# The low part of the last weight quarter made by accumulating transfers from GpSimd instead of VectorE, with the factor 4096 of the parts moved to y's side

## The chip, the cores and the metric

The kernel runs on one core of one Trainium2 chip. The metric is device time in microseconds (us) of one execution. A profiled execution also leaves a trace, whose span is the time from its first to its last instruction.

## The reference

Two blocks follow each other. The first is a Mamba-2 state-space scan over `x` of shape (4, 8, 768, 32) with decays `a` and state size 16; its output `y`, read as 3072 tokens of 256 features, is the input of the second, a feed-forward block with a hard-swish in place of a gate:

```
h = x @ w_in                      # 3072x256 @ 256x2048
g = h * np.clip(h + 3.0, 0.0, 6.0) / 6.0
out = (g @ w_out).astype(np.float32)   # 3072x2048 @ 2048x256
```

Inputs `w_in` and `w_out` arrive as 64-bit floats and are decoded to 32-bit ones on the chip.

## The kernel before, in words

The sequence is cut into six chunks of 128 positions (`NC` = 6), each with its four batches, so 512 tokens a chunk. Step `k` of the main loop runs the feed-forward block of chunk `k` and, interleaved by hand, the scan of chunk `c = k + 1` and preparations for `ahead = k + 2`. All engines work through queues in the order in which the code issues instructions; a queue stops at an instruction whose inputs are not ready, and everything behind it waits too. SyncE (SP) issues the loads and stores; GpSimd (POOL) issues no transfer.

Chunk 0 multiplies `w_in` in plain 32-bit floats (`mlp_in`). From chunk 1 on, TensorE multiplies in the faster `float32r` type, and the lost precision is brought back by parts. Each of y and `w_in` is split into a high part `hi` (a rounded, scaled copy made by ScalarE), a low part `lo` (what the rounding lost, plus a small multiple) and `less` (a combination of the two). One tile `h` of 128 features by 512 tokens is then the sum of hi·hi, lo·lo and less·less with a factor 4097 between them (`squares`, `enlarge`, `cross`). Each of the three is two products of 128x512, one for each half `j` of the 256 input features.

`w_in` has four quarters, held in tiles `w_in[0..3]` of 128 partitions by 2 x 512 floats. The generator `in_parts(i)` makes the parts of quarter `i`. Its pieces are issued by `next(ins[i])`: the first call issues the two ScalarE instructions for `hi` (L663); the second issues two VectorE instructions of 128x512 for half 0, `lo` (L666) and `less` (L669); the third the same for half 1. For quarters 0 to 2 that happens before step 1. For quarter 3 the three calls stand in step 1, after tiles f = 4, 5 and 7 of the 16 tiles of `h`. Quarter 3 serves f = 12 to 15.

In step 1, tile f goes through these pieces: `squares(f)` (TensorE, four products, hi first and then lo), `cross(f - 2)` (TensorE, two products with `less`), `enlarge(f)` (ScalarE, L711), `factor(f - 2)`, which is a ScalarE `ramp` (L730) and a VectorE product (L735) into `gT`. Six PSUM banks hold the tiles `h` in turn, so `squares(12)` needs that L735 of f = 6 is done. `conceal` (L158) issues the GpSimd selects on the decay tile `L` after f = 8 and f = 12; `weight_sums` (L776) puts VectorE sums of 128x1024 after f = 9, 11 and 13; `g_sums` (L796) issues sums of `gT` on GpSimd after f = 15. The SP queue loads for later chunks are issued around the start of step 1: `L` (L301), `eto` (L308), `xt` (L119) and `B` (L94).

`split_y(k)` makes the three parts of y: `y_hi` on ScalarE (L680), `y_lo` (L681) and `y_less` (L684) on VectorE, two instructions of 128x512 each per chunk.

Of the kernel before, what the change touches and what calls it, by code (L numbers as in the profile page):

```python
# [8 lines left out]
FP32 = mybir.dt.float32  # L9
# [4 lines left out]
AF = mybir.ActivationFunctionType  # L14
ALU = mybir.AluOpType
# [6 lines left out]
def kernel(  # L22
# [24 lines left out]
    nc = tc.nc  # L47
# [7 lines left out]
    NK = DM // P  # L55
# [30 lines left out]
    def load_bc(c):  # L86

        sl = slice(c * P, (c + 1) * P)  # L90

        def tokens_first(src, queue=nc.sync, **where):
            t = loads.tile([P, NB * NH, N], FP32, **where)
            queue.dma_start(out=t, in_=src[:, :, sl, :].rearrange("b h s n -> s (b h) n"))  # L94
            return t

        def pairs_first(src):
            t = loads.tile([P, 2, NB, 4, N], FP32, name="pairs", tag="bc")
            for b in range(NB):
                for h in range(2):  # L100
                    nc.sync.dma_start(  # L101
                        out=t[:, h, b].rearrange("s a n -> s (a n)"),
                        in_=src[b, h:NH:2, sl, :].rearrange("h (s a) n -> h s (a n)", a=4))
            return t

        if 0 < c < TURN:
            bcs[c] = [tokens_first(C, name="C", tag="bc")]
        Bs[c] = tokens_first(B, nc.scalar if c == 0 else nc.sync, name="B", bufs=1)
        if c == 0:
            bcs[c] = [pairs_first(C), Bs[c]]  # L110
        elif c < TURN:
            bcs[c].append(Bs[c])
        else:
            bcs[c] = [pairs_first(C), pairs_first(B)]

    def load_x(c):
        sl = slice(c * P, (c + 1) * P)
        xts[c] = loads.tile([P, NB * NH, D], FP32, name="xt", bufs=1)
        nc.sync.dma_start(out=xts[c], in_=x[:, :, sl, :].rearrange("b h s d -> s (b h) d"))  # L119

    NP = 4
    FP = NF // NP
    w_in = [const.tile([P, NK, FP * P], FP32, name="w_in", tag=f"w{i}") for i in range(NP)]
# [31 lines left out]
    def conceal_in(t, pattern):  # L155
# [24 lines left out]
        out=head, in_=head, pattern=[[-2 * N, NQ], [-N, 2]], compare_op=ALU.is_ge,  # L180
        fill=0.0, base=0, channel_multiplier=1)
    nc.gpsimd.affine_select(
        out=head, in_=head, pattern=[[2 * N, NQ], [N, 2]], compare_op=ALU.is_ge,
# [59 lines left out]
    less = const.tile([P, G], BF16, name="less")  # L243
# [134 lines left out]
    def conceal(c, p):  # L378
        conceal_in(Ls[c][:, 2 * p:2 * p + 2], [[0, 2], [0, NH], [1, HT]])
# [20 lines left out]
    def carry(c):  # L400

        tmps[c] = att.tile([P, NB, 2 * D], FP32, name="tmp", bufs=1)
        nc.gpsimd.tensor_tensor(  # L403
            out=tmps[c], in0=states[c - 1],
            in1=etos[c][:, :, HT - 1:HT].to_broadcast([P, NB, 2 * D]), op=ALU.mult)
# [77 lines left out]
    def turn_all(c):  # L483
        bT, _, csT = turned(c)
        for t, out_ in zip(bcs[c], (csT, bT)):
            turn_squares(t, out_)
        part_heads(c)
        fade(c)
# [150 lines left out]
    EPS = 2.0 ** -12  # L639
    w_parts, y_parts, hs_ = {}, {}, {}  # L640

    def in_parts(i):

        n = FP * P  # L650

        def one(pool, tag):
            t = pool.tile([P, NK, n], F32R, name="w_part", tag=tag)
            return [t[:, j] for j in range(NK)]

        def two(tag):
            return [att.tile([P, n], F32R, name="w_part", tag=tag) for _ in range(NK)]

        hi = one(const, f"w{i - 1}" if i > 1 else f"hi{i}")
        lo = one(const, f"lo{i}") if i < 2 else one(att, "wm") if i == 2 else two("ws")  # L660
        less = one(const, f"less{i}") if i < 2 else one(att, "wm") if i == 2 else two("we")
        for j in range(NK):
            nc.scalar.activation(hi[j], w_in[i][:, j], AF.Copy, scale=(1.0 - EPS / 2) * EPS)  # L663
        for j in range(NK):
            yield
            nc.vector.scalar_tensor_tensor(  # L666
                out=lo[j], in0=hi[j].bitcast(FP32), scalar=-1.0 / EPS, in1=w_in[i][:, j],
                op0=ALU.mult, op1=ALU.add)
            nc.vector.tensor_tensor(  # L669
                out=less[j], in0=lo[j].bitcast(FP32), in1=hi[j].bitcast(FP32), op=ALU.subtract)  # L670
        w_parts[i] = (hi, lo, less)
        yield

    def split_y(k):
        hi = const.tile([P, NK, TB], F32R, name="y_hi", tag="w0")
        lo = att.tile([P, NK, TB], F32R, name="y_lo", bufs=1)
        less = att.tile([P, NK, TB], F32R, name="y_less", bufs=1)
        for j in range(NK):
            y = yTs[k][:, j].rearrange("p b i -> p (b i)")
            nc.scalar.activation(hi[:, j], y, AF.Copy, scale=1.0 - EPS / 2)  # L680
            nc.vector.tensor_tensor(  # L681
                out=lo[:, j], in0=y, in1=hi[:, j].bitcast(FP32), op=ALU.subtract)
        for j in range(NK):
            nc.vector.scalar_tensor_tensor(  # L684
                out=less[:, j], in0=lo[:, j].bitcast(FP32), scalar=-1.0 / EPS,
                in1=hi[:, j].bitcast(FP32), op0=ALU.mult, op1=ALU.add)
        y_parts[k] = (hi, lo, less)

    def part_products(k, f, n, m, start=False):
# [6 lines left out]
    def squares(k, f, low=True):  # L696

        pool, tag = ((ps, "f0"), (ps, "f1"), (ps, "f2"), (ps, "f3"), (ps_y, "y0"), (ps_y, "y1"))[f % 6]
        hs_[k, f] = pool.tile([P, TB], FP32, name="h", tag=tag)
        part_products(k, f, 0, 0, start=True)  # L700
        if low:
            part_products(k, f, 1, 1)

    def enlarge(k, f):

        h = hs_[k, f]
        if f < 2 if k == 1 else f % 4 == 3:
            nc.vector.tensor_scalar(
                out=h, in0=h, scalar1=1.0 / EPS + 1.0, scalar2=None, op0=ALU.mult)
        else:  # L710
            nc.scalar.activation(h, h, AF.Copy, scale=1.0 / EPS + 1.0)  # L711

    def cross(k, f):
        part_products(k, f, 2, 2)

    def factor(k, f):
        ramp(k, f, hs_[k, f])
        times_ramp(k, f, hs_[k, f])
# [65 lines left out]
    def g_sums(k, j0, ops=range(4)):  # L784

        if k not in gsums:
            gsums[k] = {n: loads.tile([P, NJ, 2 * P], FP32, name=f"s{n}", tag="raw", bufs=NRAW)
                        for n in (1, 2, 4)}
        js = slice(j0, j0 + 2)
        a11, a12, a21, a22 = (g_quarter(k, e, r)[:, js] for r in range(2) for e in range(2))  # L790
        s1, s2, s4 = (gsums[k][n][:, js] for n in (1, 2, 4))
        sums_ = ((s1, a21, a22, ALU.add), (a21, a11, a21, ALU.subtract),
                 (s2, s1, a11, ALU.subtract), (s4, a12, s2, ALU.subtract))
        for n in ops:
            o, p_, q_, op = sums_[n]
            nc.gpsimd.tensor_tensor(out=o, in0=p_, in1=q_, op=op)  # L796
# [154 lines left out]
    def results(c, parts=range(2)):  # L951
        mix(c, parts)
        keep(c)
        split_y(c)
# [75 lines left out]
    for k in range(NC):  # L1030
        gTs[k] = ffn.tile([P, NF, TB], FP32, name="gT")
        c, ahead = k + 1, k + 2
        if k == 0:
# [8 lines left out]
            weights(NP + 3, 1)  # L1042
            weights(NP + 2, 3)
            sums, ins = weight_sums(), [in_parts(i) for i in range(NP)]
            next(ins[0])
            w_more = {(1, 1): (0, 0, 1), (2, 1): (1, 1, 2)}
# [37 lines left out]
        for f in range(2, NF):  # L1084
            squares(k, f)
            if f == 2:
                if c < NC:
                    load_x(c)
                    carry(c)
                if k > 0 and ahead < NC:  # L1090
                    load_bc(ahead)
            cross(k, f - 2)
            enlarge(k, f)
            factor(k, f - 2)
            if f in ((8, 12) if k == 1 else (3, 7)) and ahead < NC:
                conceal(ahead, int(f in (7, 12)))
            if f == NF - 1 and k not in gsums:
                g_sums(k, 0, ())
            if k > 1 and f in (6, 10, 14):
                g_sums(k, len(g_done.setdefault(k, [])) * 2)  # L1100
                g_done[k].append(f)
            if k == 1:
                if f in (4, 5, 7):
                    next(ins[3])
                if f in (9, 11, 13):
                    next(sums)
                if f == NF - 1:
                    turn_all(c)
# [67 lines left out]
```

## Time and profile before

| what | value |
|---|---|
| median of 3 runs | 343.59 us (343.59 to 344.37) |
| profiled execution | 343.4 us |
| its span | 341.7 us |
| busy: TensorE / VectorE / ScalarE / GpSimd | 333.8 / 210.7 / 188.3 / 145.4 us |
| `lo` of `w_in` (L666), 8 instructions | median 685 ns, up to 1627 ns |
| `less` of `w_in` (L669), 8 instructions | median 738 ns, up to 1516 ns |
| `y_lo` (L681), `y_less` (L684), 10 each | median 692 and 684 ns |
| the four selects (L158) of GpSimd in step 1 | 5.0 us busy |

The profiled execution's own time is 1.7 us longer than its span and 0.2 us under the median. A busy time is what the profiler recorded as running; idle time of an engine that is not the bottleneck costs nothing by itself.

### The profile page before, as it was taken

The page shows a single profiled execution, that of the slowest core. Times are in us where ns is not written, and L with a number is a line of the kernel's source. Part 1 is how long each engine was busy: PE and PEld are TensorE (multiplying, and loading weights), DVE is VectorE, ACT ScalarE, POOL GpSimd, SP SyncE. Part 2 cuts the span into 40 slices and gives each one's busy share as a digit, 9 for nine tenths or more (in the row PEclk, how much of TensorE's full clock was granted, in tenths as well). Part 3 has the DMA queues.
Part 4 walks back from the last instruction along what each step waited for, and adds up shares of the span by engine and source line. Part 5 has one row for each costly group of instructions (what it writes and reads, how often), then busy time and mean ns, then how long its engine had stood idle before and what let it go on. Part 6 is the DMA issues. An engine that isn't in the chain of part 4 may idle for free.

```text
span 341.7 us, 8203 instructions
## 1 busy us (share of the span) xinstructions
PE 333.8 (98%) x3372; PEld 267.5 (78%) x3372; DVE 210.7 (62%) x332; ACT 188.3 (55%) x394; POOL 145.4 (43%) x139
## 2 busy tenths in 40 slices
PE   5999999999999999999999999999999999999996
PEld 2554448888878888888888888888888888888996
DVE  6699999996499739665519465528465323465011
ACT  4778878667987481675471676470576030576000
POOL 3300000381282998099803089810089600079600
PEclk9999999999999999999999999999999999999999
DMA  8989967052690216167107294001260001110000
GB/s 172 174 312 197 209 233 153 2 59 69 164 114 8 58 55 119 25 84 70 24 27 144 33 96 62 16 2 18 33 75 2 2 4 17 30 17 2 0 33 31
DMA packets 89605, 25.15 MB, mean 74 GB/s; under 512 B 82208, under 2 KB 85952, under 8 KB 89056
## 3 DMA queue, kind: packets, MB, share of 16 engines
q1 hardware_dynamic: 85184, 23.33, 36.5%
q10 hardware_dynamic: 4384, 1.31, 1.8%
q8 instruction: 26, 0.43, 0.5%
q14 instruction: 11, 0.09, 0.1%
HBM read 21.33 MB, written 3.29 MB: 72 GB/s over the span
## 4 chain that ended last, share of the span: by engine, by line
PE 94%; DMA 3%; DVE 1%; SPq 1%; issue 0%; DVEq 0%
PE h L692 33%; PE wb L874 13%; PE wc L874 8%; PE o L748 8%; PE h L626 8%; PE wa L874 8%; PE oa L810 4%; PE ob L810 4%; PE y L604 3%; PE y L503 2%; PE cb L530 2%; DMA raw<-in_moe_w_in_dram 2%; PE y L544 1%; DMA pairs<-in_C_dram 1%; SPq L101 1%; DVE L L574 0%
## 5 line engine op out<-in xcount | busy, mean ns | idle before, releaser
L735 DVE SCALAR_TENSOR_TENSOR gT<-gT,h 128x512 f32<-128x512 f32 x96 | 64.9, 686 | 41.1 <-ACT gT L730 39.9
L730 ACT ACTIVATE gT<-h,half 128x512 f32<-128x512 f32 x96 | 65.2, 684 | 17.8 <-PE h L692 15.9
L796 POOL TENSOR_TENSOR s<-gT 128x512 f32<-128x512 f32 x20 | 28.9, 1443 | 76.2 <-DVE gT L735 76.1
L711 ACT ACTIVATE h<-h 128x512 f32<-128x512 f32 x62 | 35.8, 583 | 43.6 <-PE h L692 39.3
L692 PE MATMUL h<-y_hi,w_part 128*128 128x512 f32 x160 | 51.8, 409 | 0.0
L692 PE MATMUL h<-y_less,w_part 128*128 128x512 f32 x160 | 49.7, 397 | 0.0
L692 PE MATMUL h<-y_lo,w_part 128*128 128x512 f32 x160 | 49.5, 395 | 0.0
L692 PEld LDWEIGHTS h<-y_lo,w_part 128*128 128x128 f32 x160 | 30.0, 188 | 7.4
L692 PEld LDWEIGHTS h<-y_less,w_part 128*128 128x128 f32 x160 | 30.0, 188 | 6.9
L692 PEld LDWEIGHTS h<-y_hi,w_part 128*128 128x128 f32 x160 | 30.0, 188 | 6.8 <-DVE gT L735 0.4
L385 ACT ACTIVATE L<-L,cum_n 128x64 f32<-128x64 f32 x128 | 31.6, 338 | 0.0
L874 PE MATMUL wb<-s,w_out 128*128 128x256 f32 x128 | 30.6, 382 | 0.0
L748 PE MATMUL o<-w_out,gT 128*128 128x256 f32 x128 | 28.8, 381 | 0.0
L626 PE MATMUL h<-yT,w_in 128*128 128x512 f32 x64 | 27.7, 594 | 0.0
L748 PEld LDWEIGHTS o<-w_out,gT 128*128 128x128 f32 x128 | 24.1, 190 | 3.8 <-issue 0.5
L403 POOL TENSOR_TENSOR tmp<-state,eto 128x256 f32<-128x256 f32 x5 | 3.4, 673 | 55.3 <-ACT eto L389 55.2
L874 PEld LDWEIGHTS wb<-s,w_out 128*128 128x128 f32 x128 | 24.0, 190 | 3.6
L796 POOL TENSOR_TENSOR s<-gT,s 128x512 f32<-128x512 f32 x20 | 26.0, 1306 | 1.3
L796 POOL TENSOR_TENSOR gT<-gT 128x512 f32<-128x512 f32 x20 | 25.7, 1291 | 1.3
L796 POOL TENSOR_TENSOR s<-s,gT 128x512 f32<-128x512 f32 x20 | 25.7, 1290 | 0.0
L158 POOL TENSOR_SCALAR_AFFINE_SELECT L<-L 64x1024 f32<-64x1024 f32 (+1 forms) x16 | 20.4, 1280 | 10.5 <-DMA L<-cum_d 10.1
L396 POOL TENSOR_TENSOR bs<-B,L 128x128 f32<-128x128 f32 x24 | 12.7, 545 | 26.0 <-ACT L L385 20.9
(138 smaller groups left out, 507.5 us busy)
## 6 DMA issues: line engine op xcount, KB each, us to landing
raw<-in_moe_w_out_dram SPq DMA_DIRECT2D x4, 1024.0 KB
L<-cum_d SPq DMA_DIRECT2D x8, 512.0 KB
xt<-in_x_dram SPq DMA_DIRECT2D x6, 512.0 KB
raw<-in_moe_w_in_dram SPq DMA_DIRECT2D x3, 1024.0 KB
out_dram<-back SPq DMA_DIRECT2D x128, 16.0 KB
pairs<-in_C_dram SPq DMA_DIRECT2D x40, 32.0 KB
eto<-cum_e SPq DMA_DIRECT2D x20, 64.0 KB
B<-in_B_dram SPq DMA_DIRECT2D x5, 256.0 KB
```

Of the source, the lines that this page charges most:

```text
L158: nc.gpsimd.affine_select(out=t[rows], in_=t[rows], pattern=pattern, compare_op=ALU.is_ge, fill=-1e5, base=base, channel_multiplier=-1)
L385: nc.scalar.activation(Ls[c][:, b, h], Ls[c][:, b, h], AF.Exp, bias=cum_n[:, c, g:g + 1])
L396: nc.gpsimd.tensor_tensor(out=bss[c][:, hs], in0=Bs[c][:, hs], in1=Ls[c][:, b, :, HT - 1:HT].to_broadcast([P, NH, N]), op=ALU.mult)
L626: nc.tensor.matmul(out=h, lhsT=w_in[f // FP][:, j, f % FP * P:(f % FP + 1) * P], rhs=yTs[k][:, j].rearrange("p b i -> p (b i)"), start=(j ...
L692: nc.tensor.matmul(out=hs_[k, f], lhsT=w[j][:, f % FP * P:(f % FP + 1) * P], rhs=y[:, j], start=(start and j == 0), stop=True, skip_group_ ...
L711: nc.scalar.activation(h, h, AF.Copy, scale=1.0 / EPS + 1.0)
L730: nc.scalar.activation(gTs[k][:, f], h, AF.Relu, bias=half, scale=1.0 / 6.0)
L735: nc.vector.scalar_tensor_tensor(out=g, in0=g, scalar=1.0, in1=h, op0=ALU.min, op1=ALU.mult)
L748: nc.tensor.matmul(out=o[:, b % 2], lhsT=gTs[0][:, f, b * P:(b + 1) * P], rhs=w_out[:, f], start=(f == 0 and b % 2 == 0), stop=True, skip_ ...
L796: nc.gpsimd.tensor_tensor(out=o, in0=p_, in1=q_, op=op)
L810: nc.tensor.matmul(out=bank[:, slot], lhsT=lhs[:, j], rhs=rhs[:, j], start=(clear and j == 0), stop=True, skip_group_check=True)
L874: nc.tensor.matmul(out=bank[:, slot], lhsT=lhs[:, j], rhs=rhs[:, j], start=(clear and j == 0), stop=True, skip_group_check=True)
```

## The change

For `w_in`, `hi` is now the negative of the rounded weight without the factor 2^-12, so that `lo` is a plain sum of the weight and `hi`; the factor 2^-12 is on `y_hi` instead. `less` takes the multiplication by 4096. For y the two VectorE forms change places in the same way. Quarters 0 to 2 do the plain sum on VectorE (`tensor_tensor`). For quarter 3, GpSimd issues two transfers that add `hi` into `w_in[3]` in place (one for each half) and two more that copy the sums into `lo`, all after tile f = 4; the two `less` are issued after f = 10 and f = 11.

```diff
         for j in range(NK):
-            nc.scalar.activation(hi[j], w_in[i][:, j], AF.Copy, scale=(1.0 - EPS / 2) * EPS)
+            nc.scalar.activation(hi[j], w_in[i][:, j], AF.Copy, scale=EPS / 2 - 1.0)
+        for j in range(NK if i == NP - 1 else 0):
+            nc.gpsimd.dma_start(
+                out=w_in[i][:, j], in_=hi[j].bitcast(FP32), accum_op=ALU.add)
+        for j in range(NK if i == NP - 1 else 0):
+            nc.gpsimd.dma_start(out=lo[j], in_=w_in[i][:, j])
         for j in range(NK):
             yield
+            if i < NP - 1:
+                nc.vector.tensor_tensor(
+                    out=lo[j], in0=w_in[i][:, j], in1=hi[j].bitcast(FP32), op=ALU.add)
             nc.vector.scalar_tensor_tensor(
-                out=lo[j], in0=hi[j].bitcast(FP32), scalar=-1.0 / EPS, in1=w_in[i][:, j],
-                op0=ALU.mult, op1=ALU.add)
-            nc.vector.tensor_tensor(
-                out=less[j], in0=lo[j].bitcast(FP32), in1=hi[j].bitcast(FP32), op=ALU.subtract)
+                out=less[j], in0=lo[j].bitcast(FP32), scalar=-1.0 / EPS, in1=hi[j].bitcast(FP32),
+                op0=ALU.mult, op1=ALU.subtract)
...
         for j in range(NK):
             y = yTs[k][:, j].rearrange("p b i -> p (b i)")
-            nc.scalar.activation(hi[:, j], y, AF.Copy, scale=1.0 - EPS / 2)
+            nc.scalar.activation(hi[:, j], y, AF.Copy, scale=(EPS / 2 - 1.0) * EPS)
+            nc.vector.scalar_tensor_tensor(
+                out=lo[:, j], in0=hi[:, j].bitcast(FP32), scalar=1.0 / EPS, in1=y, op0=ALU.mult,
+                op1=ALU.add)
+        for j in range(NK):
             nc.vector.tensor_tensor(
-                out=lo[:, j], in0=y, in1=hi[:, j].bitcast(FP32), op=ALU.subtract)
-        for j in range(NK):
-            nc.vector.scalar_tensor_tensor(
-                out=less[:, j], in0=lo[:, j].bitcast(FP32), scalar=-1.0 / EPS,
-                in1=hi[:, j].bitcast(FP32), op0=ALU.mult, op1=ALU.add)
+                out=less[:, j], in0=lo[:, j].bitcast(FP32), in1=hi[:, j].bitcast(FP32), op=ALU.add)
...
             if k == 1:
-                if f in (4, 5, 7):
+                if f in (4, 10, 11):
                     next(ins[3])
```

On GpSimd's queue the four transfers stand behind the `tmp` product (L403) of step 1 and ahead of the four selects of `conceal`. Each copy waits until the addition of its own half has landed. `squares(12)` now waits for the copies, and so do the two `less`. The third `weight_sums`, which writes over the buffer of `w_in[3]`, waits for the additions as well.

## The prediction

> **What bounds the kernel now.** I read the page first, for the shares and for the chain that ended last.
>
> ```profile
> PE 333.8 (98%) x3372; PEld 267.5 (78%) x3372; DVE 210.7 (62%) x332; ACT 188.3 (55%) x394; POOL 145.4 (43%) x139
> ...
> PE h L692 33%; PE wb L874 13%; PE wc L874 8%; PE o L748 8%; PE h L626 8%; PE wa L874 8%; PE oa L810 4%; PE ob L810 4%; PE y L604 3%; PE y L503 2%; PE cb L530 2%; DMA raw<-in_moe_w_in_dram 2%; PE y L544 1%; DMA pairs<-in_C_dram 1%; SPq L101 1%; DVE L L574 0%
> ```
>
> TensorE carries the chain nearly alone, so the change is worth what it does to TensorE's waits. Next, the chain in order of time around step 1 (start, length, what), and TensorE's weight loads there.
>
> ```profile
> 85.07 14.85 PE h L692 x64
> 99.92 0.02 issue
> 99.94 6.30 PE h L692 x26
> ```
>
> ```profile
> 99.07 0.42 PEld L692 LDWEIGHTS h<-y_less,w_part 128*128 128x128 f32 x2
> 99.94 0.30 PEld L692 LDWEIGHTS h<-y_hi,w_part 128*128 128x128 f32 x2 [0.45 <-DVE gT L735]
> ```
>
> The 64 products from 85.07 are four `lo` of tiles 0 and 1 and six for each of f = 2 to 11, 232 ns each. The break at 99.94 is therefore the start of `squares(12)`. It waited for L735 of f = 6 to free its bank. That is the only stall here: the 26 products after it take 6.30 us where 26 x 0.232 is 6.03. VectorE was late because of this:
>
> ```profile
> 93.69 0.69 DVE L666 SCALAR_TENSOR_TENSOR w_part<-w_part,w_in 128x512 fp32r<-128x512 f32 x1
> ...
> 96.21 1.53 DVE L666 SCALAR_TENSOR_TENSOR w_part<-w_part,w_in 128x512 fp32r<-128x512 f32 x1
> 97.78 1.51 DVE L669 TENSOR_TENSOR w_part<-w_part 128x512 fp32r<-128x512 f32 x1
> 99.21 1.27 DVE L735 SCALAR_TENSOR_TENSOR gT<-gT,h 128x512 f32<-128x512 f32 x2
> ```
>
> Then what the new transfers meet: ScalarE's `hi`, GpSimd's selects, SP's issues, and the DMA share by stretches (each windows row ends with granted clock, DMA share, GB/s).
>
> ```profile
> 90.81 1.15 ACT L663 ACTIVATE w_part<-w_in 128x512 fp32r<-128x512 f32 x2
> ```
>
> ```profile
> 92.36 1.14 POOL L158 TENSOR_SCALAR_AFFINE_SELECT L<-L 64x1024 f32<-64x1024 f32 x1 [5.09 <-DMA L<-cum_d]
> 94.90 3.86 POOL L158 TENSOR_SCALAR_AFFINE_SELECT L<-L 128x1024 f32<-128x1024 f32 x3 [1.39 <-DMA L<-cum_d]
> ```
>
> ```profile
> 87.56 1.15 SPq L301 DMA_DIRECT2D L<-cum_d  x2
> ...
> 91.38 0.46 SPq L119 DMA_DIRECT2D xt<-in_x_dram  x1
> 91.95 5.71 SPq L94 DMA_DIRECT2D B<-in_B_dram  x1
> ```
>
> ```profile
> 88.00:92.00 4.00, 4.00 (x19) 3.25 (x18) 2.06 (x3) 3.56 (x8) 0.00 (x0) 1.00 0.99 265
> 92.00:96.00 4.00, 4.00 (x19) 3.24 (x18) 2.88 (x5) 3.91 (x8) 2.25 (x2) 1.00 1.21 177
> 96.00:102.00 6.00, 5.98 (x26) 4.52 (x26) 5.96 (x7) 4.86 (x9) 5.80 (x5) 1.00 1.10 100
> 102.00:106.00 4.00, 4.00 (x19) 3.25 (x18) 4.00 (x6) 3.35 (x7) 1.55 (x2) 1.00 0.00 0
> ```
>
> The engines are full from 88 to about 101 us, exactly while the new transfers must run; SP needs 5.71 us to issue `B`.
>
> **The change: what it removes.** Two L666, 0.69 + 1.53 = 2.2 us of VectorE, and the two L669 leave their places ahead of L735 of f = 4 and 6. L735 of f = 6 can then follow its ScalarE ramp (ends 96.5) and frees the bank by about 97.3. TensorE starts `squares(12)` at 99.76, and its wait of 0.3 us (6.30 - 6.03 + 0.02) is gone. Nothing more can be gained: from 85 to 135 us the chain has no other stall of that size.
>
> **What only changes form.** Quarters 0 to 2 and y swap a SCALAR_TENSOR_TENSOR with a TENSOR_TENSOR: 685 against 738 ns (medians) for the weights, 684 against 692 for y, counts equal. `y_lo` is ready 2 us before its product at 85.07 and, in step 1, at 130.1 against 135.7. Zero.
>
> **What moves on GpSimd and SP.** The four selects (1.14 + 3.86 = 5.0 us) now stand behind the copies, hence behind the landing of the additions; they end near 104 instead of 98.7. Behind them stand the sums of `gT`: two that took 98.73 to 102.78, one at 105.22, and one at 111.86 that waits for VectorE anyway. Three sums of up to 2.2 us after 104 still end by 110.6. ScalarE first needs the selects at 110.9. SP's `xt` and `B` share the engines with 1 MB more, but are used at 121.9 and 129.5, and SP then idles until 108.5. Zero, unless the copies land after about 105.
>
> **What is added to the path.** `squares(12)` needs `lo` of half 0 at 100.2 (99.76 + two `hi` products) and of half 1 at 100.5. `hi` is ready at 91.4 and 92.0. In between, each half crosses two dependent transfers of 256 KB. No row shows GpSimd issuing one, so I bound a hop by the nearest rows.
> - Low end: the load of `a` (96 KB, issued at 0.80) releases VectorE at 3.97; less 0.25 us for its bytes at the 363 to 393 GB/s of that stretch, 2.9 us are fixed. 256 KB at 321 GB/s (88 to 90 us) add 0.8. Additions land at 95.1 and 95.9, copies at 98.8 and 99.6: in time.
> - Middle row: the two `L` loads themselves, 1 MB, are in at 94.90, so 1 MB in 94.90 - 87.56 - 2.9 = 4.4 us, 1.1 us for 256 KB. Sharing with SP's queue, 2.2 us. Additions land at 96.5 and 98.7, copies at 101.6 and 103.8.
> - High end: half of 177 GB/s, 3.0 us per transfer on top of 2.9, one queue for all. Additions land at 97.3 and 100.3, copies at 103.2 and 106.2.
>
> I take the midpoint of the ends for half 1, 102.9: SP's queue is full of packets under 512 B (82208 of 89605 in the run), so an even share is the best that I can assume, but its backlog thins towards 101. Before, the product with half 1 started at 100.75. The loss is 102.9 - 100.75 = 2.15 us; that already counts the 0.3 us won back. While TensorE waits, everything behind waits, and nothing later has slack to give back, since the chain is TensorE to 338.5 us.
>
> VectorE's new wait is milder than TensorE's: by ScalarE's ramps, `less` of half 0 comes up at about 100.5, after L735 of f = 8 and a sum of 1.2 us. Behind it queue L735 of f = 9 and on, `less` of half 1 and two sums. `squares(15)` needs the bank of f = 9, `cross(12)` needs both `less`; both come 3.7 us or more after the start of `squares(12)` (16 products), which is itself held by the same landing. Two instructions of 0.7 us fit: zero.
>
> Sum: 343.4 + 2.15 = 345.55 against the profiled execution, which lies 0.2 under the median: 345.7.
>
> **The rivals.**
> - *In time.* The low end holds, half 1 lands before 100.5, TensorE never waits, and the banks' 0.3 us is won: 343.3; "same" reaches to landings at 101.8, where the loss is 1.03 us. For it: 2 KB rows inside one core's memory, not the small packets that slow SP. Against it: DMA shares of 1.21 and 1.10, and two hops in 8.5 us. [...]
> - *Much too late.* An addition reads both operands; if it then takes twice the high end's 3.0 us, half 1 lands at 112 with SP's backlog unchanged, and at about 108 as that thins: a loss of 7.3 us, 350.9. At the high end alone it is 349.0. For it: full engines. Against: SP's backlog ends near 101. All rows have the clock at 1.00, with no gap on TensorE this long. [...]
> - *Faster.* VectorE's relief would have to remove over 1 us of waits in step 1. The chain shows only 0.3 us.
>
> **How the numbers follow.** A measurement of this kernel can tell about 0.3%, 1.03 us. The ends put the landing of half 1 between 99.6 and 106.2; 4.4 of these 6.6 us lie after 101.8, 0.67 of the way; I take 0.60, since large rows inside the memory speak for the low end. Late by 1 to 4 us: 0.45 (345.7). Much too late: 0.15. In time or nearly: 0.36. Faster: 0.04. So slower 0.60, same 0.36, faster 0.04. The range takes in the rival in time (343.0, just under 343.3) and the high end (349.0, to 349.5 with a part of its side effects).
>
> **What would show it.** Right: a gap on TensorE before the `lo` products of f = 12, released by a transfer, of about 2 us; the h products from 85 us without the wait on L735; the first select at 97 us or later; y's parts unchanged. Wrong: the copies landing before 100.5 with no gap (then a hop costs under 4.3 us), a gap over 5 us, or a delay in the sums of `gT` that reaches the `wb` products at 120 us.

## The result, and the profile after

The changed kernel takes 352.11 us (median of 4 runs, 351.26 to 352.6) against 343.59: 1.0242 times the time before, 95% interval 1.0223 to 1.026, or 8.5 us slower. The profiled execution took 352.6 us with a span of 350.9. Beside the kernel before on a second chip the ratio was 1.0256 (1.0233 to 1.028).

First the page of the changed kernel (line numbers are 7 higher behind the edit).

```profile
PE 336.0 (96%) x3372; PEld 268.8 (77%) x3372; DVE 209.4 (60%) x330; ACT 188.5 (54%) x394; POOL 148.9 (42%) x143
...
q0 software_dynamic: 576, 1.05, 1.7%
```

TensorE has the same 3372 products, VectorE its two instructions fewer, GpSimd its four transfers more, on a queue of their own (q0). Next, the chain in order of time through step 1.

```profile
86.26 4.66 PE h L699 x20
...
92.95 8.05 DMA w_in<-w_part
...
101.30 0.56 POOL w_part L669
...
102.72 5.19 DMA w_part<-w_in
107.91 0.04 issue
107.96 7.16 PE h L699 x23
115.11 1.73 PE wa L881 x8
```

Where two runs of products stood before with 0.02 us between them, the chain now leaves TensorE for 17 us: `hi`, the addition, GpSimd's issue, the copy. The addition shown is that of half 0 and the copy that of half 1: GpSimd's timeline has it wait 0.86 us, until about 102.7, for the addition of half 1 before it issues this copy. The landing times of the pairs are in the DMA view (columns: tile, queue, count, size, median us from issue to landing).

```profile
w_in<-w_part POOLq DMA_DIRECT2D x2, 256.0 KB, 8.4
w_part<-w_in POOLq DMA_DIRECT2D x2, 256.0 KB, 5.3
```

TensorE's timeline at f = 12, the duration running from the first start to the last end of a row's products, which overlap:

```profile
100.95 0.63 PE L699 MATMUL h<-y_hi,w_part 128*128 128x512 f32 x2
106.82 0.80 PE L699 MATMUL h<-y_lo,w_part 128*128 128x512 f32 x1 [5.24 <-DMA w_part<-w_in]
107.96 0.79 PE L699 MATMUL h<-y_lo,w_part 128*128 128x512 f32 x1 [0.34 <-DMA w_part<-w_in]
108.55 1.05 PE L699 MATMUL h<-y_less,w_part 128*128 128x512 f32 x2
```

The `hi` products start on time, and then TensorE stands for 5.24 us until the first half is copied. After the gap each product takes 0.43 us instead of 0.23 (rows 0.85 us apart instead of 0.46). The windows view gives the reason in its third column from the right:

```profile
92.00:96.00 4.00, 4.00 (x19) 3.24 (x18) 2.02 (x3) 4.00 (x9) 1.96 (x2) 1.00 1.05 188
96.00:102.00 6.00, 5.58 (x25) 4.17 (x23) 3.85 (x6) 5.13 (x9) 0.56 (x1) 1.00 1.45 182
102.00:106.00 4.00, 0.00 (x0) 0.00 (x0) 0.00 (x0) 0.00 (x0) 3.20 (x4) 0.82 1.45 166
106.00:110.00 4.00, 2.84 (x6) 1.95 (x7) 3.20 (x4) 0.94 (x2) 3.93 (x3) 0.50 0.16 40
110.00:114.00 4.00, 4.00 (x16) 3.21 (x15) 3.22 (x4) 2.74 (x5) 3.01 (x3) 0.82 0.00 0
```

The granted clock is 0.50 from 106 to 110 and mixed on both sides. The DMA share is 1.05 to 1.45 from 92 to 106, nearly all the time in which the transfers run.

The span's 9.2 us divide like this. From the start of the `lo` products of f = 0 to the `wa` products it is 28.85 us (115.11 - 86.26) against 21.17: 7.68 us, and the same 7.68 us still stand at the `h` products of the next chunk. Of them the wait makes 5.1 (the first `lo` product of f = 12 stands 20.56 us behind that start, before 15.45); the rest, 2.6 us, falls between the first `lo` product and `wa`: the second half's own wait (0.9 us: the two `lo` products start 1.14 us apart instead of 0.23) and the half clock. Another 0.3 us come behind the last product. The other 1.2 us lie ahead of step 1, 1.0 of them at a pause of TensorE at about 20.3 us that waits for nothing the profile shows. It was 0.17 us before and 1.14 us after, but 1.23 us in a kernel without any of the transfers and 0.02 us in one with them (both below): it goes with the execution, not with the edit.

### The profile page after: what moved, and what is told of

Read it like the earlier page. It is cut to its first block, busy times and chain, and to the rows that moved or that the text cites. A ratio compares the mean times of both kernels' runs of the same rounds, so it can differ in the third digit from the quotient of the medians.

```text
span 350.9 us, 8209 instructions
## 1 busy us (share of the span) xinstructions
PE 336.0 (96%) x3372; PEld 268.8 (77%) x3372; DVE 209.4 (60%) x330; ACT 188.5 (54%) x394; POOL 148.9 (42%) x143
## 3 DMA queue, kind: packets, MB, share of 16 engines
q0 software_dynamic: 576, 1.05, 1.7%
## 4 chain that ended last, share of the span: by engine, by line
PE 89%; DMA 7%; DVE 1%; issue 1%; SPq 1%; ACT 0%; POOL 0%; DVEq 0%; POOLq 0%
PE h L699 29%; PE wb L881 12%; PE wc L881 8%; PE o L755 8%; PE h L626 8%; PE wa L881 8%; PE oa L817 4%; PE ob L817 4%; PE y L604 3%; DMA w_in<-w_part 2%; PE y L503 2%; PE cb L530 2%; DMA raw<-in_moe_w_in_dram 2%; DMA w_part<-w_in 1%; PE y L544 1%; DMA pairs<-in_C_dram 1%
## 5 line engine op out<-in xcount | busy, mean ns | idle before, releaser
L699 PE MATMUL h<-y_lo,w_part 128*128 128x512 f32 x160 | 50.9, 403 | 5.6 <-DMA w_part<-w_in 5.6
L403 POOL TENSOR_TENSOR tmp<-state,eto 128x256 f32<-128x256 f32 x5 | 3.4, 673 | 56.2 <-ACT eto L389 56.1
L626 PEld LDWEIGHTS h<-yT,w_in 128*128 128x128 f32 x64 | 12.1, 190 | 14.9 <-issue 12.9
```

Source lines behind the costliest of these rows:

```text
L626: nc.tensor.matmul(out=h, lhsT=w_in[f // FP][:, j, f % FP * P:(f % FP + 1) * P], rhs=yTs[k][:, j].rearrange("p b i -> p (b i)"), start=(j ...
L699: nc.tensor.matmul(out=hs_[k, f], lhsT=w[j][:, f % FP * P:(f % FP + 1) * P], rhs=y[:, j], start=(start and j == 0), stop=True, skip_group_ ...
```

## The experiments

**The new forms without the transfers.** All quarters add up on VectorE:

```diff
-        for j in range(NK if i == NP - 1 else 0):
-            nc.gpsimd.dma_start(... accum_op=ALU.add)
-        for j in range(NK if i == NP - 1 else 0):
-            nc.gpsimd.dma_start(out=lo[j], in_=w_in[i][:, j])
...
-            if i < NP - 1:
+            if True:
...
-                if f in (4, 10, 11):
+                if f in (4, 5, 7):
```

> No transfers from GpSimd: all four quarters add up on VectorE, with the signs, the factor and the forms of the changed kernel, and the three calls for quarter 3 back at f = 4, 5 and 7. If the transfers are the whole loss, 343.6 (within 0.3%) and the h products of step 1 as before. If the changed forms (TENSOR_TENSOR for lo, SCALAR_TENSOR_TENSOR for less, on w and y) cost anything, it shows here: two more nanoseconds each would be nothing, 1 us or more would need a new wait on VectorE's parts.

Ratio to the kernel before 1.0001 (0.9968 to 1.0035). Its chain has step 1 in one piece:

```profile
86.37 21.14 PE h L694 x90
```

Before, the same 90 products took 21.17 us. Signs, factor and forms cost nothing that the chain or the interval (1.2 us either way) can show, so the loss comes with the transfers.

**SP's loads moved down in the code.**

```diff
             lead_on(c)
-            rows(ahead + 1)
...
+            if k == 1 and f == 13:
+                rows(ahead)
+                load_x(c)
+                load_bc(ahead)
```

> The changed kernel with SP's loads of L, eto, xt and B moved from the start of step 1 to after f = 13, and the selects on L to after f = 15, so that the four transfers have the DMA engines to themselves. Theory A (traffic): an addition lands in 3 to 5 us instead of 8.0, the copies by 99 us, no gap on TensorE at f = 12, 343.3 to 344. Theory B (an addition is slow by itself): still about 8 us each, copies at 104 to 107, a gap of 3 to 5 us, 348 to 352.

1.0241 (1.0182 to 1.03), additions 8.4 us, like the changed kernel. But the experiment did not do what it was meant to: SP's queue in this run shows

```profile
88.29 1.16 SPq L301 DMA_DIRECT2D L<-cum_d  x2
...
92.71 6.20 SPq L94 DMA_DIRECT2D B<-in_B_dram  x1
```

L301 starts 2.5 us behind the first `lo` product of step 1, as in the changed kernel (88.76 there). In both runs SP issued L301 0.11 us behind the end of its store of `ob` (L761: 88.18 us here, 88.65 there): a place further down among other engines' instructions did not hold it. The run says nothing about traffic.

**The additions made plain copies.**

```diff
-                out=w_in[i][:, j], in_=hi[j].bitcast(FP32), accum_op=ALU.add)
+                out=w_in[i][:, j], in_=hi[j].bitcast(FP32))
```

> The changed kernel with the two additions made plain copies of the same bytes between the same places (the addition itself is left out). Everything else, SP's loads beside them included, is as it was. If adding in the transfer is what costs (theory B), the first pair lands in 5.3 us like the second pair, the copies are in by about 101, the gap on TensorE is 0 to 1 us and the time 343.5 to 345. If the traffic of SP's loads costs it (theory A), the first pair still takes about 8 us and the time stays near 352.

351.02 us (one run). The DMA view:

```profile
w_in<-w_part POOLq DMA_DIRECT2D x2, 256.0 KB, 7.5
w_part<-w_in POOLq DMA_DIRECT2D x2, 256.0 KB, 5.0
```

Without adding, the first pair still takes 7.5 us beside SP's loads, 0.9 less than with it, and TensorE still stands for 3.8 us. Adding is a small part of the cost; the theory that it is the whole falls.

**SP's loads really held back.** A small store on SP that reads the last copied half stands ahead of them:

```diff
+                if f == 4:
+                    nc.sync.dma_start(out=held, in_=lows[3][1].bitcast(FP32)[:1, :16])
+                    rows(ahead)
+                    load_x(c)
+                    load_bc(ahead)
```

with the two `conceal` after f = 15.

> The changed kernel with SP's loads of L, eto, xt and B held back until the copies have landed (a 64-byte store on SP that reads the last copied half stands ahead of them), and the selects on L after f = 15. The four transfers have the DMA engines to themselves at the same place in step 1. Theory A: additions in about 4 us (as in the earlier start, 4.2), copies in 3 to 4, half 1 by 100, gap 0 to 1 us, 343.5 to 345. Theory B: 8 us each for the additions, 348 to 352. A loss of its own would be the late loads: xt is needed at 115 us, L's selects by 111.

Ratio 1.0021 (1.0007 to 1.0035), 344.85 against 343.93 us. The transfers, at the same place in step 1, and the chain:

```profile
w_in<-w_part POOLq DMA_DIRECT2D x2, 256.0 KB, 3.9
w_part<-w_in POOLq DMA_DIRECT2D x2, 256.0 KB, 2.3
```

```profile
85.31 20.89 PE h L702 x90
```

Theory A holds: with the engines to themselves the two hops take 3.9 and 2.3 us, there is no gap, and step 1 is 0.28 us shorter than before (20.89 against 21.17): the wait for a bank, and all that there was to win. GpSimd's issue of the two additions takes 1.96 us of its queue here as in the changed kernel, so it is what follows the issue that the traffic draws out. The kernel still comes out slightly slower, most likely since the selects wait for the late `L` and GpSimd's last sums run beside y's third part, seen in the timelines of VectorE and GpSimd:

```profile
129.82 3.42 DVE L695 TENSOR_TENSOR y_less<-y_lo,y_hi 128x512 fp32r<-128x512 f32 x2
```

```profile
127.63 6.74 POOL L806 TENSOR_TENSOR s<-gT,s 128x512 f32<-128x512 f32 x4
```

Before, these two `y_less` took 1.72 us and the four sums began at 124.13 and took 5.42. That the late sums slow `y_less` is read from the overlap, not tested by itself. TensorE then waits 0.9 us for VectorE at 133 us.

**Only `xt` and `B` held back** (as above, without `rows(ahead)`; the selects as in the changed kernel).

> Only xt and B (rows of 128 and 64 bytes) held back until the copies have landed; L and eto stay where they are. If the many small rows are what slows the additions, they land in 4 to 5 us and the gap is under 1.5 us (344 to 345.5). If the 1.25 MB of L and eto, which go out first, are, the additions stay at 7 to 8 us and only the copies get faster (3.5 us instead of 5.3), gap about 3 us: 347 to 349, with less or no halved clock.

346.04 us (one run).

```profile
w_in<-w_part POOLq DMA_DIRECT2D x2, 256.0 KB, 6.2
w_part<-w_in POOLq DMA_DIRECT2D x2, 256.0 KB, 2.6
```

So both kinds of load count: `L` and `eto` add 2.3 us to an addition (6.2 against 3.9), `xt` and `B` another 2.2 (8.4) and 2.7 to a copy (5.3 against 2.6). The gap here is 1.3 us, and the granted clock stays at 1.00 in every window. The expectation had 4 to 5 us if the small rows were the cause and 7 to 8 us, at 347 to 349, if the large ones were; 6.2 lies between the two.

**The transfers started earlier.** `next(ins[3])` right after the parts of y for chunk 1, about 8.6 us earlier as seen from the first `lo` product of step 1; `less` after f = 5 and 7, or after f = 10 and 11:

```diff
                     elif (i, b) == (3, 1):
                         results(c)
+                        next(ins[3])
...
-                if f in (4, 10, 11):
+                if f in (5, 7):
```

> The changed kernel with the first call for quarter 3 (ScalarE's hi and the four transfers) some 8 us earlier, right after the parts of y for chunk 1, and the two less after f = 5 and f = 7. Under both theories the copies land before 100 us (A: about 90 to 92; B: 96 to 99), so no gap at f = 12 and the clock stays at 1.00: 343.2 to 344. Under A the additions, which run in a stretch of low DMA share, land in under 5 us; under B still in 8. If the less on VectorE at f = 5 and 7 have to wait for copies as late as B has them, VectorE stands still and squares(12) waits for a bank: 344 to 346.

> The early start of the transfers (after the parts of y for chunk 1) with the two less after f = 10 and f = 11, so that VectorE never waits for a copy (it waited 2.4 us with less at f = 5). If nothing else is lost, the chain has no gap in step 1 and no wait for a bank at f = 12: 0.3 us under the kernel before, 343.3 to 343.8 on this chip, same within 0.3%. If the early start costs elsewhere (ScalarE's 1.2 us ahead of the decays of the next chunk, GpSimd's sums kept waiting behind the transfers), 344.5 to 346.

Ratios 1.0042 (1.0009 to 1.0076) and 1.0037 (1.0019 to 1.0054). The additions land in 4.2 and 4.0 us where the engines are not full, the copies in 5.8 and 4.8 once SP's loads have begun; no product of f = 12 waits for them. So some 7 of the 8.5 us come back by an earlier issue alone. Neither wins: TensorE's timeline of the second has a new wait,

```profile
114.95 0.70 PE L881 MATMUL wb<-gT,t 128*128 128x256 f32 x2 [1.18 <-DVE gT L742]
```

for the last `gT` from VectorE. Taking the two `less` from f = 5 and 7 to 10 and 11 did not cure it, so VectorE's wait for the copies was not the whole reason. VectorE's timeline of this run shows longer instructions: its sums at 99.63 and 104.75 take 2.12 and 2.31 us and the two `less` 1.02 each, where the run with SP's loads held back has 1.22 for each sum and 0.68 for each `less`. These 2.7 us are more than the wait. GpSimd runs its selects and sums beside them here (99.5 to 110.5), and stands idle in the held run (97.9 to 104.9). But before the change a sum of VectorE took 1.21 us beside sums of GpSimd, so an overlap alone does not always do it, and the cause stays open.

**TensorE kept busy through the gap.** Products on the identity between the `hi` and the `lo` products of f = 12, first nine, then seven:

```diff
         part_products(k, f, 0, 0, start=True)
+        if k == 1 and f == 12:
+            busy(7, ps_o.tile([P, NB * P], FP32, name="fill", tag="o"))
```

> The changed kernel with nine products on the identity (4.7 us at full clock) between the hi and the lo products of f = 12, where TensorE stands still for 5.2 us: nothing waits for them. If the stall alone costs the time, 352.1 as the changed kernel. If the halved clock after the gap costs its own 1.7 us (products from 108.5 to 111.5 at about 0.43 us instead of 0.23), the granted clock stays at 1.00 and it is 350.2 to 350.5.

> As the run with nine filler products, which took 0.86 us each and ended 1.3 us after the copy had landed, but with seven (6.0 us, over before the copies land). Clock theory: TensorE is kept busy through the gap, the granted clock stays at 1.00, the 23 products after it run at 0.232 us, and it is 1.6 to 1.8 us faster than the changed kernel beside it. If the stall alone counts, equal to the changed kernel.

> The changed kernel unaltered, on the same chip as the seven fillers, for the comparison: 8.5 us over the kernel before, granted clock 0.99.

The nine took 7.72 us instead of the 4.7 I had reckoned (they multiply in plain 32-bit floats, in 18 pieces of 0.43 us at full clock) and ended 1.3 us after the second copy had landed: 1.029 (1.0219 to 1.0362). The seven fit: 352.37 us against 352.86 for the changed kernel beside it (ratios to before 1.0239 and 1.0256, intervals overlapping). The granted clock is full:

```profile
106.00:110.00 4.00, 3.71 (x14) 2.25 (x13) 3.52 (x4) 1.52 (x3) 3.93 (x4) 1.00 0.11 32
```

In TensorE's timelines it is 5.45 us from the second half's `lo` product to `wa` (113.17 - 107.72), against 7.10 in the changed kernel beside it (114.74 - 107.64): the half clock costs 1.65 us there. From the `lo` products of f = 0 on, 1.36 us of it are won (27.66 against 29.02), since the second half landed 0.3 us later in this run. At the `h` products of the next chunk only 0.8 us are left; the medians differ by 0.5 us, the two profiled spans by 0.2. VectorE has become the chain, as the chain of the seven shows:

```profile
106.48 1.63 DVE w_part L675
...
108.71 1.11 DVE w_part L675
109.82 1.11 DVE t L785
...
118.69 1.21 DVE gT L744 x2
119.94 0.70 PE wb L883 x2
```

It had stood at `less` for the same copies, and its backlog of `less`, sums and `gT` holds the last `wb` products for 0.4 us. So a part of what the clock costs is hidden behind VectorE; how much of the rest reaches the end, these few runs cannot tell.

## Why the prediction was wrong

The direction and the place were right: a gap on TensorE ahead of the `lo` products of f = 12, released by the copy, and nothing on the side of forms. The size was not: 345.7 forecast, range to 349.5, 352.1 measured. The prediction's own sign of being wrong, "a gap over 5 us", is what came.

The step that failed is the landing of half 1, "the midpoint of the ends, 102.9". On the old time scale it landed at 106.7 (107.9 less the 1.2 us by which step 1 starts later), past the high end of 106.2. These 3.8 us are the largest part of the 6.4 us between 345.7 and 352.1. The low end was right about an empty machine: 3.7 us a hop against 3.9 and 2.3 measured with SP held back, and two hops of together 6.2 us would have been in time. The error was in the share. I wrote that an even share with SP's queue is the best that can be assumed, and still gave the low end, in which the share is all, half the weight. The addition took 8.05 us, where the high end with an even share had 5.9; the copy 5.2, between the middle row's 5.1 and the high end's 5.9. Only the additions meet SP's whole backlog (8.4, 6.2 and 3.9 us beside all of the loads, `L` and `eto`, and none; the copies 5.3, 2.6 and 2.3). That half 1 still came only 0.5 us past the high end is luck in part: the high end had the two halves 3.0 us apart, one behind the other, and they landed 1.1 us apart.

The second miss is an omission. The rows of before have the clock at 1.00, and the sum has no term for it; the stall of 5.24 us is followed by products at half speed (0.43 us instead of 0.23), and that made about 1.6 us of step 1. The last microsecond is not all accounted for: 0.3 us lie behind the last product, and the early pause differs from execution to execution. The rival "much too late" had the landing at 108 and 350.9 without the clock: nearer, though its reason, an addition that pays for reading both operands, does not hold: the plain copies are only 0.9 us faster (7.5 against 8.4).

By the other steps: 0.3 us to win by the freed bank, and no more, was right (0.28, with SP held back). "Zero" for the changed forms was right. "Zero" for VectorE's new wait holds in the changed kernel, whose chain through step 1 does not pass VectorE, but there was no margin: with the clock kept up it is the next limit. "Zero" for the selects was right in the changed kernel, where they are done at 108.5 behind a stall, and doubtful as a margin: with the selects later still they most likely cost the 0.9 us at 133 us. One reading was wrong without effect: `xt` is used from 114.78 on (L544), not from 121.9.

No version tried is faster than the kernel before. The most there is to win in step 1 is 0.28 us, 0.08%, less than the intervals here can show.

## What to carry to other kernels

Before work is moved from an engine to transfers, look at the DMA share of the very stretch where they must run, count dependent hops, and price a hop at what a transfer costs in that traffic, not in an empty machine: here 13 us for two hops instead of 6. Where a wait on a saturated TensorE may be as long as here (3.8 us halved the clock, 1.3 us did not), put the products at half clock into the sum, but check first which engine is late next, since it may hide some of the same microseconds. And a load is held back by a dependence, not by its place in the code: moved down, L301 still began at 88.29 us (88.76 in the changed kernel), behind the small store at 99.99.

## What the runs showed of the hardware

- Four transfers of 256 KB from GpSimd in SBUF: 3.9 us (adding) and 2.3 us (copying) from issue to landing with the DMA engines otherwise idle, 8.4 and 5.3 us beside SP's loads. GpSimd needs about 1 us of its queue for the issue of an adding one (1.96 for two), 0.64 for a plain one, 0.55 for the copy into `float32r`.
- The granted clock: a gap of 1.3 us left it at 1.00, gaps of 3.8 and 5.2 us brought 0.50. From the windows' means in the changed kernel it fell at about 104.6 (0.82 over 102 to 106), 3.0 us after TensorE's last product ended at 101.6, and was back at about 111.4 (0.82 over 110 to 114), 4.6 us after work came back. With windows of half a microsecond the stretch at 0.50 is 6.8 us long there. In its repeat, the plain copies and the loads moved down, the means of the windows on both sides (0.81 and 0.84, 0.72 and 0.93, 0.79 and 0.85, with 0.50 between them) give 6.8 to 6.9 us too, whether TensorE had stood for 3.8 or for 5.3 us. What sets this length was not shown.
